# Loading, casting and transposing the first q, k group in two halves of 64 partitions

## The chip, the cores and the metric

The kernel runs on one core of one Trainium2 chip. The metric is the device time of one execution in microseconds (us); lower is better. The core has five engines with an instruction queue each: PE (TensorE, matmuls and transposes; its weight loads are shown apart as PEld), DVE (VectorE), ACT (ScalarE), POOL (GpSimd) and SP (SyncE, which issues transfers). Each engine runs its own instructions in order, and semaphores hold one engine until another has done its part.

## The reference

The reference is a block-causal attention followed by a feed-forward layer with a maximum of two branches. q, k and v have 8 batches, 8 heads, 576 positions and 64 features.

```python
def _attn_ref(q, k, v):
    B, H, S, D = q.shape                      # 8, 8, 576, 64
    block = 64
    scale = 1.0 / np.sqrt(D)
    scores = scale * np.matmul(q, k.transpose(0, 1, 3, 2))
    ...
    mask = block_i >= block_j                 # by blocks of 64 positions
    scores = np.where(mask, scores, -1000000000.0)
    ...
    attn = np.exp(scores)                     # softmax over the keys
    attn = attn / (np.sum(attn, axis=-1, keepdims=True) + 1e-09)
    return np.matmul(attn, v)

def _moe_ref(x, w1, w2, w_out):               # x: 4608 x 512
    return np.maximum(x @ w1, x @ w2) @ w_out # 512 -> 1024 -> 512
```

## The kernel before

**Units of work.** Two heads make a pair, and there are 32 pairs (`NPAIR`). Two pairs, that is four heads of one batch, make a group; there are 16 groups. A group's q and k are loaded as one tile each of 128 partitions: the partition index is `(h p)`, with `h` (0 or 1) choosing the pair and `p` running over 64 partitions, each of which holds 9 (`RPP`) consecutive positions of each of the pair's two heads. So partitions 0 to 63 belong to the first pair of the group and 64 to 127 to the second. A tile holds 1152 fp32 values in each partition.

**From q and k to scores.** `load_qk` (L89) issues the two loads of a group. `cast` (L101) turns the fp32 tile into bf16 tiles `qn` and `kn`, and its list `parts` says which engine takes which of the 9 columns. `transposes` (L259) transposes 64 x 128 pieces on PE, nine for each pair, into two PSUM tiles, and gives back a function that copies these to the SBUF tiles `qT` and `kT` of the two pairs (L272). `scores` (L278) multiplies kT by qT for the two heads of a pair.

**A pair.** `burst_a` (L295) computes two PSUM tiles of scores and issues their exponentials on ACT (L288) and block masks on POOL (L293). `burst_b` (L306) does the other two. There are two score buffers in PSUM (`ps_s`), so the first tile of burst_b waits for the first exponential of burst_a, and so on. `av` (L317) multiplies the exponentials by v and normalises on DVE, `x_out` (L345) transposes the result into `xT`, and `h_unit` and `y_unit` are the feed-forward layer, whose matmuls are dealt out by `fill` between the attention work of later pairs.

**Buffers in PSUM.** All transposes, warm-up matmuls, av and feed-forward tiles take turns in one pool of four buffers (`ps_m`, tag "m"), in the order in which the program asks for them. A tile waits until the reader of the buffer's previous tile is done.

**Order.** The order is written out by hand. The start is: the loads of groups 0, 1 and 2 from SP and ACT; memsets on DVE; the casts of group 0, split between DVE, POOL and ACT (L145, L146); three v loads on POOL, the q cast of group 1 on POOL (L149), two more v loads and four weight loads on POOL. On PE, `warm_up(16)` issues 16 matmuls on zeros, then come the 36 transposes of q and k of group 0 (L418, L419), `warm_up(3)`, and the four copies that feed the first two pairs (L421 to L424). Then the loop over the first four pairs (L425) runs: burst_a, some other work and warm-ups, burst_b. For pair 0 the other work is the k cast of group 1 on DVE and `warm_up(4)` after burst_a, and the q transposes of group 1 and `warm_up(2)` after burst_b. Steady state, with the feed-forward work mixed in, begins after these four pairs.

Of the kernel before, what the change touches and what calls it, by code (L numbers as in the profile page):

```python
# [8 lines left out]
FP32 = mybir.dt.float32  # L9
BF16 = mybir.dt.bfloat16  # L10
# [4 lines left out]
def kernel(  # L15
# [10 lines left out]
    nc = tc.nc  # L26

    B, H, S, D = q.shape
    P = 128
# [13 lines left out]
    NP = 64  # L43
    RPP = S // NP
# [17 lines left out]
    raw = ctx.enter_context(tc.tile_pool(name="raw", bufs=4))  # L62
    qkn = ctx.enter_context(tc.tile_pool(name="qkn", bufs=2))
# [4 lines left out]
    ps_m = ctx.enter_context(tc.tile_pool(name="ps_m", bufs=4, space=bass.MemoryType.PSUM))  # L68
# [5 lines left out]
    qT_r = [ring.tile([P, S], BF16, name=f"qT{r}") for r in range(NT)]  # L74
    kT_r = [ring.tile([P, S + APAD], BF16, name=f"kT{r}") for r in range(NT)]
# [6 lines left out]
    ident = wpool.tile([P, P], BF16, name="ident")  # L82


    raws = {}
    qk_n = {}
    dve, pool, act = nc.vector.tensor_copy, nc.gpsimd.tensor_copy, nc.scalar.copy

    def load_qk(g, queues, gated=False):  # L89
        b, u = divmod(g, GPB)  # L90
        for nm, src, queue in (("q", q, queues[0]), ("k", k, queues[1])):
            raws[nm, g] = t = raw.tile([P, 2, RPP * D], FP32, name=f"{nm}raw")
            if gated:
                nc.gpsimd.memset(t[:, 0, :1], 0.0)
            queue.dma_start(
                out=t[:],
                in_=src[b, 4 * u:4 * u + 4].rearrange(
                    "(s h) (p t) d -> (h p) s (t d)", h=2, t=RPP),
            )

    def cast(nm, g, parts):  # L101
        t = raws.pop((nm, g)).rearrange("p s (t d) -> p t s d", d=D)
        qk_n[nm, g] = n = qkn.tile([P, RPP, 2, D], BF16, name=f"{nm}n")
        for copy, j0, j1 in parts:
            copy(out=n[:, j0:j1], in_=t[:, j0:j1])  # L105
# [20 lines left out]
    dve, pool, act = nc.vector.tensor_copy, nc.gpsimd.tensor_copy, nc.scalar.copy  # L126
    SP, ACT = nc.sync, nc.scalar
    warm = small.tile([P, 1], FP32, name="warm")
    load_qk(0, (SP, ACT))
    nc.vector.memset(warm[:], 0.0)  # L130
    zeros = wpool.tile([P, SPAN], BF16, name="zeros")
    nc.vector.memset(zeros[:], 0.0)  # L132
# [9 lines left out]
    for r in range(NA):  # L142
        nc.vector.memset(aT_r[r][BLK:, :, CB[4] + 512:], 0.0)
        nc.vector.memset(aT_r[r][:BLK, :, AW:], 0.0)
    cast("q", 0, ((dve, 0, 6), (pool, 6, RPP)))  # L145
    cast("k", 0, ((act, 0, 5), (dve, 5, RPP)))  # L146
    for c in range(3):
        load_v(0, c)
    cast("q", 1, ((pool, 0, RPP),))  # L149
    for c in range(3, NCH):  # L150
        load_v(0, c)
# [99 lines left out]
    def warm_up(n):  # L251
        pw = ps_m.tile([P, SPAN], FP32, name="ps_w", tag="m")
        for _ in range(n):
            nc.tensor.matmul(pw[:], zeros[:, :P], zeros[:], start=True, stop=True)  # L254
# [4 lines left out]
    def transposes(nm, g, copies):  # L259
        n = qk_n.pop((nm, g))  # L260
        pts = [ps_m.tile([P, RPP, NP], BF16, name=f"ps_{nm}T", tag="m") for _ in range(2)]
        for j in range(RPP):
            for i in range(2):
                r = slice(i * NP, (i + 1) * NP)
                nc.tensor.transpose(  # L265
                    pts[i][:, j, :], n[r, j].rearrange("p s d -> p (s d)"), ident[r, r],
                )

        def copy_out(which=(0, 1)):
            for i in which:  # L270
                t = (qT_r if nm == "q" else kT_r)[(2 * g + i) % NT]
                copies[i](  # L272
                    out=t[:, :S].rearrange("q (p j) -> q p j", j=RPP),
                    in_=pts[i].rearrange("q j p -> q p j"),
                )
        return copy_out
# [18 lines left out]
    def burst_a(p):  # L295
        u0 = ps_s.tile([P, 2, 512], FP32, name="ps_s", tag="s")
        scores(p, u0, 0, 0, 0, 512)
        u1 = ps_s.tile([P, 2, 512], FP32, name="ps_s", tag="s")
        scores(p, u1, 0, 0, 512, 64)
        scores(p, u1, 64, 1, 128, 448)  # L300
        exp(p, u0, 512, 0)
        mask(p, 0)
        exp(p, u1, 512, 512)
        mask(p, 576)

    def burst_b(p):  # L306
        u2 = ps_s.tile([P, 2, 512], FP32, name="ps_s", tag="s")
        scores(p, u2, 0, 2, 256, 320)
        scores(p, u2, 320, 3, 384, 192)
        u3 = ps_s.tile([P, 2, 512], FP32, name="ps_s", tag="s")  # L310
        scores(p, u3, 0, 4, 512, 64)
        exp(p, u2, 512, 1024)
        mask(p, 1024)
        mask(p, 1344)
        exp(p, u3, 64, 1536, m=BLK)

    def av(p, ts):  # L317
        b, hp = divmod(p, HP)
        vv = vv_r[b % NV]
        a = aT_r[p % NA]  # L320
        n = len(ts)
        h0 = hp // 2 * 4 + hp % 2
        if p % 2 == 0 and ts[0] == 0:
            xps[p // 2] = xpool.tile([P, NCH, 2, 2, D], BF16, name="xp")
        xp = xps[p // 2]
        po = ps_m.tile([P, n, 2, D + 1], FP32, name="ps_o", tag="m")
        n_mm = 2 * sum(t + 1 for t in ts)
        mm = 0
        for gi, t in enumerate(ts):
            for hh in range(2):  # L330
                for c in range(t + 1):
                    a0 = CB[c] + t * P
                    nc.tensor.matmul(  # L333
                        po[:, gi, hh, :], a[:, hh, a0:a0 + P], vv[:, c, h0 + 2 * hh, :],
                        start=(mm == 0), stop=(mm == n_mm - 1),
                    )
                    mm += 1
        rec = small.tile([P, 3, 2, 1], FP32, name="rec")
        nc.vector.reciprocal(rec[:, :n, :, 0], po[:, :, :, D])  # L339
        nc.vector.tensor_mul(  # L340
            xp[:, ts[0]:ts[0] + n, :, p % 2], po[:, :, :, :D],
            rec[:, :n].to_broadcast([P, n, 2, D]),
        )
# [24 lines left out]
    def fill_of(s):  # L368
        if s >= NPAIR - LAG:
            return 27  # L370
        left = 10 - s if s < 10 else 4 - (s - 2) % 4
        return -(-max(0, ready() - KEEP) // left)


    def pool_work(s):
        g, i = divmod(s, 2)
        if s == 0:
            load_w(512, 512)
            load_qk(3, (SP, SP), gated=True)
        elif s == 1 or s == 2:  # L380
            pass
        elif s == 3:
            cast("q", 2, ((act, 0, RPP),))
            cast("k", 2, ((act, 0, RPP),))
            load_qk(4, (SP, SP), gated=True)
            for c in range(3):
                load_v(1, c)
            cast("q", 3, ((pool, 0, RPP),))
            cast("k", 3, ((pool, 0, RPP),))
            for c in range(3, NCH):  # L390
                load_v(1, c)
            load_wo(0, 4)
            load_wo(4, 4)
        elif s == 4:
            pass
        elif s == 5:
            load_qk(5, (SP, SP), gated=True)
            cast("q", 4, ((pool, 0, RPP),))
        else:
            if i == 1 and g + 3 < NG:  # L400
                load_qk(g + 3, (SP, SP), gated=True)
            if g + 1 + i < NG:
                cast("kq"[i], g + 1 + i, ((pool, 0, RPP),))
            nb, j = divmod(s + 2, HP)
            if nb < B:
                for c in ((0, 1), (2, 3), (4,), ())[j]:
                    load_v(nb, c)
# [7 lines left out]


    warm_up(16)
    cq = transposes("q", 0, (dve, act))  # L418
    ck = transposes("k", 0, (act, dve))  # L419
    warm_up(3)  # L420
    cq((0,))  # L421
    ck((0,))
    cq((1,))
    ck((1,))  # L424
    for s in range(HP):  # L425
        burst_a(s)
        if s == 0:
            cast("k", 1, ((dve, 0, RPP),))
            warm_up(4)
        elif s == 1:  # L430
            transposes("k", 1, (dve, dve))()
            warm_up(2)
        elif s == 2:
            av(0, [0, 1])
            warm_up(2)
        else:
            av(0, [2, 3, 4])
        burst_b(s)
        pool_work(s)
        if s == 0:  # L440
            transposes("q", 1, (dve, dve))()
            warm_up(2)
        elif s == 1:
            warm_up(4)
        elif s == 2:
            warm_up(3)
# [8 lines left out]
    for s in range(HP, NPAIR):  # L455
# [3 lines left out]
        n = fill_of(s)  # L459
        if s == HP:  # L460
            fill(6)
            cq = transposes("q", 2, (dve, act))
            ck = transposes("k", 2, (dve, act))
# [11 lines left out]
        if s >= HP + LAG:  # L475
            p = s - LAG
# [53 lines left out]
```

The softmax here doesn't subtract the row's maximum and nothing guards it: scores larger than these inputs give would overflow.

## Time and profile before

| | |
|---|---|
| median of 7 executions | 294.28 us (293.65 to 294.82) |
| the profiled execution, its own time | 294.85 us |
| its span, first to last instruction | 293.1 us |
| PE busy | 277.8 us, 95% of the span |
| DVE, ACT, POOL busy | 181.8, 140.2, 95.8 us |
| granted TensorE clock | 1.00 |
| first scores on PE, first exponential on ACT | 9.62 us, 10.05 us |
| first feed-forward matmul | 28.9 us |

The profile is of one execution. Times in its timeline count from the first instruction of the span. A row gives the start, the time from first to last of the merged instructions, the engine, the line, the operation, what it writes and reads, and in brackets the idle time ahead of it with the instruction or transfer that ended it. Engines overlap, so busy times do not add up to the span. A busy PE is not a PE at its peak rate, because matmuls are pipelined.

### The profile page before, as it was taken

What the parts mean: (1) busy time and instruction counts of PE and PEld (TensorE: products, weight loads), DVE (VectorE), ACT (ScalarE), POOL (GpSimd) and SP (SyncE); (2) the same over time, 40 slices, a digit from 0 to 9 for tenths busy, and PEclk for the clock granted to TensorE, in tenths of its full rate; (3) what the DMA queues carried; (4) which work ended last, traced back from release to release, by engine and by line L of the source; (5) the groups of instructions that cost most, each with busy time, mean ns of one, the idle gap of its engine ahead of it and who ended that gap; (6) DMA issues with size and microseconds to landing.
All of it is one profiled execution on the core that took longest, in us unless ns stands there. A gap on an engine that the chain in (4) does not pass through costs nothing.

```text
span 293.1 us, 7406 instructions
## 1 busy us (share of the span) xinstructions
PE 277.8 (95%) x3067; PEld 141.3 (48%) x3116; DVE 181.8 (62%) x363; ACT 140.2 (48%) x200; POOL 95.8 (33%) x236
## 2 busy tenths in 40 slices
PE   8777999999999999999999999999999999999995
PEld 2445445555555454445444545454554544444443
DVE  6627767546987676756666666666665766464530
ACT  3784587576655555554555555545555000101112
POOL 3956536725553443144324432443111000000000
PEclk9999999999999999999999999999999999999999
DMA  7999999957934792568656494455110111011104
GB/s 268 284 195 284 227 168 178 218 146 176 201 25 157 81 228 45 200 73 206 77 197 73 113 171 136 83 65 66 43 38 37 38 60 49 36 72 38 72 36 143
DMA packets 56081, 36.65 MB, mean 125 GB/s; under 512 B 38768, under 2 KB 43376, under 8 KB 56048
## 3 DMA queue, kind: packets, MB, share of 16 engines
q0 software_dynamic: 41728, 7.87, 33.4%
q1 hardware_dynamic: 13760, 27.60, 27.6%
q10 hardware_dynamic: 560, 0.72, 0.8%
q8 instruction: 24, 0.39, 0.6%
q14 instruction: 9, 0.07, 0.1%
HBM read 34.60 MB, written 9.44 MB: 150 GB/s over the span
## 4 chain that ended last, share of the span: by engine, by line
PE 90%; ACT 4%; DVE 3%; issue 2%; ACTq 0%
PE ps_h L168 42%; PE ps_y L186 20%; PE ps_o L333 11%; PE ps_s L282 8%; ACT aT L288 3%; PE ps_w L254 3%; PE ps_qT L265 2%; PE ps_kT L265 2%; PE ps_xe L353 2%; DVE xp L340 1%; PE ps_y L203 1%; DVE kT L272 1%; DVE xT L358 0%; DVE qT L272 0%; DVE rec L339 0%
## 5 line engine op out<-in xcount | busy, mean ns | idle before, releaser
L168 PE MATMUL ps_h<-xT,w_sb 128*128 128x512 bf16 x547 | 133.6, 379 | 3.5 <-issue 1.7
L288 ACT ACTIVATE aT<-ps_s 128x1024 bf16<-128x1024 f32 (+1 forms) x128 | 99.2, 832 | 53.6 <-PE ps_s L282 53.6
L168 PEld LDWEIGHTS <-w_sb 128*128 128x128 bf16 x576 | 51.8, 98 | 59.7 <-issue 6.1
L175 DVE CAST h<-ps_h 128x512 bf16<-128x512 f32 x72 | 49.7, 691 | 44.9 <-PE ps_h L168 43.6
L186 PE MATMUL ps_y<-wo_sb,g 128*128 128x512 bf16 x262 | 66.5, 379 | 1.0 <-issue 0.2
L293 POOL MEMSET aT<- 64x128 bf16 x128 | 23.7, 200 | 121.9 <-ACT aT L288 121.7
L192 ACT COPY y<-ps_y 128x512 f32<-128x512 f32 x35 | 20.5, 587 | 83.9 <-PE ps_y L186 56.8
L177 DVE TENSOR_TENSOR g<-h,ps_h 128x512 bf16<-128x512 bf16 x72 | 49.3, 685 | 10.2 <-PE ps_h L168 10.2
L333 PEld LDWEIGHTS <-aT 128*128 128x128 bf16 x960 | 33.6, 98 | 14.9 <-DVE xp L340 8.4
L333 PE MATMUL ps_o<-vv,aT 128*128 128x65 bf16 x960 | 39.7, 194 | 1.1 <-DVE xp L340 0.4
L186 PEld LDWEIGHTS <-g 128*128 128x128 bf16 x280 | 25.5, 98 | 27.9 <-issue 3.2
L282 PE MATMUL ps_s<-qT,kT 64*128 64x64 bf16 (+4 forms) x384 | 34.4, 275 | 3.3 <-ACT aT L288 3.2
L109 POOL DMA_DIRECT2D vv<-in_v_dram x40 | 33.7, 848 | 0.3 <-issue 0.3
L340 DVE TENSOR_TENSOR xp<-ps_o,rec 128x256 bf16<-128x256 f32 x64 | 31.4, 491 | 2.2
L282 PEld LDWEIGHTS <-kT 64*128 64x128 bf16 x384 | 16.5, 94 | 18.9 <-issue 13.2
L339 DVE RECIPROCAL rec<-ps_o 128x4 f32<-128x4 f32 x64 | 11.8, 185 | 18.9 <-PE ps_o L333 18.8
L105 POOL CAST qn<-qraw 128x1152 bf16<-128x1152 f32 (+1 forms) x15 | 17.1, 1138 | 4.5 <-DMA qraw<-in_q_dram 4.4
L272 DVE COPY qT<-ps_qT 128x576 bf16<-128x576 bf16 x17 | 12.8, 757 | 7.2 <-PE ps_qT L265 6.0
L358 DVE COPY xT<-ps_xe 128x640 bf16<-128x640 bf16 x16 | 7.8, 490 | 12.4 <-PE ps_xe L353 12.1
L272 DVE COPY kT<-ps_kT 128x576 bf16<-128x576 bf16 x17 | 12.8, 757 | 4.3 <-PE ps_kT L265 3.2
L105 POOL CAST kn<-kraw 128x1152 bf16<-128x1152 f32 x13 | 14.9, 1145 | 1.6 <-DMA kraw<-in_k_dram 0.8
L254 PE MATMUL ps_w<-zeros 128*128 128x512 bf16 x34 | 11.7, 480 | 1.9 <-DVE zeros L132 1.2
(39 smaller groups left out, 103.0 us busy)
## 6 DMA issues: line engine op xcount, KB each, us to landing
qraw<-in_q_dram SPq DMA_DIRECT2D x16, 576.0 KB, 4.1
out_dram<-y SPq DMA_DIRECT2D x35, 256.0 KB, 2.1
kraw<-in_k_dram SPq DMA_DIRECT2D x15, 576.0 KB, 5.5
vv<-in_v_dram POOLq DMA_DIRECT2D x32, 128.0 KB, 5.9
w_sb<-in_moe_w_dram POOLq DMA_DIRECT2D x4, 256.0 KB, 8.2
w_sb<-in_moe_w_dram POOLq DMA_DIRECT2D x2, 512.0 KB, 16.2
wo_sb<-in_moe_w_out_dram POOLq DMA_DIRECT2D x2, 512.0 KB, 11.2
kraw<-in_k_dram ACTq DMA_DIRECT2D x1, 576.0 KB, 5.3
```

Of the source, the lines that this page charges most:

```text
L105: copy(out=n[:, j0:j1], in_=t[:, j0:j1])
L109: nc.gpsimd.dma_start(out=vv_r[b % NV][:rows, c, :, :D], in_=v[b, :, c * P:c * P + rows, :].rearrange("h p d -> p h d"),)
L168: nc.tensor.matmul(pt[:], w_sb[:, c, f * P:(f + 1) * P], xT[:, c, t0:t0 + SPAN], start=(c == 0), stop=(c == NDM - 1),)
L175: nc.vector.tensor_copy(out=h1[:], in_=pt[:])
L177: nc.vector.tensor_max(g[:, f, :], h1[:], pt[:])
L186: nc.tensor.matmul(py[:], g[:, f, s * P:(s + 1) * P], wo_sb[:, f, :], start=(f == 0), stop=(f == NFF - 1),)
L272: copies[i](out=t[:, :S].rearrange("q (p j) -> q p j", j=RPP), in_=pts[i].rearrange("q j p -> q p j"),)
L282: nc.tensor.matmul(ps[:m, hh, col:col + w], kT[r, c * P:c * P + m], qT[r, q0:q0 + w], start=True, stop=True,)
L288: nc.scalar.activation(out=aT_r[p % NA][:m, :, a0:a0 + w], in_=ps[:m, :, :w], func=AF.Exp, scale=scale,)
L293: nc.gpsimd.memset(aT_r[p % NA][BLK:, :, a0:a0 + BLK], 0.0)
L333: nc.tensor.matmul(po[:, gi, hh, :], a[:, hh, a0:a0 + P], vv[:, c, h0 + 2 * hh, :], start=(mm == 0), stop=(mm == n_mm - 1),)
L340: nc.vector.tensor_mul(xp[:, ts[0]:ts[0] + n, :, p % 2], po[:, :, :, :D], rec[:, :n].to_broadcast([P, n, 2, D]),)
```

## The change

The first group is no longer handled by `load_qk`, `cast` and `transposes`, but by three functions of its own, which treat the two pairs (`h` = 0 and 1, partitions 0 to 63 and 64 to 127) one after the other. The loads become four transfers of 64 partitions each, in the order q h=0 (SP), k h=0 (ACT), q h=1 (SP), k h=1 (ACT). The casts of h=0 keep the split of before. The q cast of h=1 goes to POOL, ahead of the v loads, and the k cast of h=1 to DVE, behind the copy of the first qT. Only the transposes of h=0 stay ahead of the first scores; those of h=1 move behind burst_a of pair 0. Each takes one PSUM buffer instead of two, and the copy of the second qT moves from ACT to DVE.

```diff
+    def load_first():
+        t = {nm: raw.tile([P, 2, RPP * D], FP32, name=f"{nm}raw") for nm in "qk"}
+        for h in range(2):
+            for nm, src, queue in (("q", q, nc.sync), ("k", k, nc.scalar)):
+                queue.dma_start(
+                    out=t[nm][h * NP:(h + 1) * NP],
+                    in_=src[0, :4].rearrange("(s h) (p t) d -> h p s (t d)", h=2, t=RPP)[h],
+                )
...
+    def cast_first(nm, h, parts):
...
+        r = slice(h * NP, (h + 1) * NP)
+        for copy, j0, j1 in parts:
+            copy(out=n[r, j0:j1], in_=t[r, j0:j1])
+
+    def transposes_first(nm, h, copy):
...
+        pt = ps_m.tile([P, RPP, NP], BF16, name=f"ps_{nm}T", tag="m")
+        for j in range(RPP):
+            nc.tensor.transpose(
+                pt[:, j, :], n[r, j].rearrange("p s d -> p (s d)"), ident[r, r])
+        t = (qT_r if nm == "q" else kT_r)[h]
+        copy(
+            out=t[:, :S].rearrange("q (p j) -> q p j", j=RPP),
+            in_=pt.rearrange("q j p -> q p j"),
+        )
...
-    load_qk(0, (SP, ACT))
+    load_first()
...
-    cast("q", 0, ((dve, 0, 6), (pool, 6, RPP)))
-    cast("k", 0, ((act, 0, 5), (dve, 5, RPP)))
+    cast_first("q", 0, ((dve, 0, 6), (pool, 6, RPP)))
+    cast_first("k", 0, ((act, 0, 5), (dve, 5, RPP)))
+    cast_first("q", 1, ((pool, 0, RPP),))
     for c in range(3):
         load_v(0, c)
     cast("q", 1, ((pool, 0, RPP),))
...
     warm_up(16)
-    cq = transposes("q", 0, (dve, act))
-    ck = transposes("k", 0, (act, dve))
+    transposes_first("q", 0, dve)
+    transposes_first("k", 0, act)
+    cast_first("k", 1, ((dve, 0, RPP),))
     warm_up(3)
-    cq((0,))
-    ck((0,))
-    cq((1,))
-    ck((1,))
     for s in range(HP):
         burst_a(s)
         if s == 0:
+            transposes_first("q", 1, dve)
+            transposes_first("k", 1, dve)
             cast("k", 1, ((dve, 0, RPP),))
             warm_up(4)
```

The second argument of `cast_first` and `transposes_first` is the half `h` of group 0; that of `cast` is the group.

More of the change, by code (lines that the diff above doesn't have):

```diff
@@ L99, in load_qk @@
             )
+    def load_first():
[6 more added lines that the diff above has]
+                )
+        for nm in "qk":
+            raws[nm, 0] = t[nm]
+            qk_n[nm, 0] = qkn.tile([P, RPP, 2, D], BF16, name=f"{nm}n")
+    def cast_first(nm, h, parts):
+        t = raws[nm, 0].rearrange("p s (t d) -> p t s d", d=D)
+        n = qk_n[nm, 0]
+        r = slice(h * NP, (h + 1) * NP)
+        for copy, j0, j1 in parts:
+            copy(out=n[r, j0:j1], in_=t[r, j0:j1])
+    def transposes_first(nm, h, copy):
+        n = qk_n[nm, 0]
+        r = slice(h * NP, (h + 1) * NP)
+        pt = ps_m.tile([P, RPP, NP], BF16, name=f"ps_{nm}T", tag="m")
[7 more added lines that the diff above has]
+        )
     def cast(nm, g, parts):
```

## The prediction

> **What bounds the kernel now.** I read the page first, then the chain of waits, then the timeline of the first 24 us. The page says that PE carries the run as a whole:
>
> ```profile
> PE 277.8 (95%) x3067; PEld 141.3 (48%) x3116; DVE 181.8 (62%) x363; ACT 140.2 (48%) x200; POOL 95.8 (33%) x236
> PE 90%; ACT 4%; DVE 3%; issue 2%; ACTq 0%
> ```
>
> The change touches only the first dozen microseconds. PE runs its instructions in a fixed order, so a shift that survives the start moves the whole run by as much. No row behind the start waits for a transfer long enough to hold it: the first MoE matmul waits at 28.86 us for the DVE copy of xT, and its weights, issued at 11.96 us with about 7 us to land, are there long before. So the question is one shift in microseconds, read from the timeline (start, duration, engine, work):
>
> ```profile
> 1.23 6.43 PE L254 MATMUL ps_w<-zeros 128*128 128x512 bf16 x16 [1.23 <-DVE zeros L132]
> ...
> 5.71 0.56 DVE L105 CAST qn<-qraw 128x768 bf16<-128x768 f32 x1
> 5.74 0.89 POOL L105 CAST qn<-qraw 128x384 bf16<-128x384 f32 x1 [4.43 <-DMA qraw<-in_q_dram]
> ...
> 6.19 0.73 DVE L105 CAST kn<-kraw 128x512 bf16<-128x512 f32 x1
> ...
> 6.58 2.77 POOL L109 DMA_DIRECT2D vv<-in_v_dram  x3
> ...
> 7.59 0.44 PE L265 MATMUL ps_qT<-ident,qn 64*128 64x64 bf16 x18
> ...
> 8.06 0.76 DVE L272 COPY qT<-ps_qT 128x576 bf16<-128x576 bf16 x1 [1.15 <-PE ps_qT L265]
> ...
> 8.32 0.64 ACT L272 COPY kT<-ps_kT 128x576 bf16<-128x576 bf16 x1 [1.52 <-PE ps_kT L265]
> ...
> 8.88 0.81 PE L254 MATMUL ps_w<-zeros 128*128 128x512 bf16 x2 [0.58 <-DVE qT L272]
> ...
> 9.33 1.18 POOL L105 CAST qn<-qraw 128x1152 bf16<-128x1152 f32 x1
> 9.40 1.34 DVE L105 CAST kn<-kraw 128x1152 bf16<-128x1152 f32 x1
> ...
> 9.62 0.61 PE L282 MATMUL ps_s<-qT,kT 64*128 64x512 bf16 x6
> ```
>
> The reader is to see three things. First, q has landed by 5.74 and all casts of the first group end by 6.92 (6.19 + 0.73), yet the transposes start at 7.59, when the 16 warm-up matmuls let PE go (1.23 + 6.43 = 7.66). An earlier load gains nothing at this point. Second, the first scores (9.62) stand behind three more warm-up matmuls on PE, and those begin at 8.88 because they need a PSUM buffer that the copy of qT frees (8.06 + 0.76 = 8.82). Third, POOL goes from its part of the cast through three v loads to the q cast of group 1, which ends at 9.33 + 1.18 = 10.51. From the first scores on, PE and ACT alternate:
>
> ```profile
> 10.05 3.00 ACT L288 ACTIVATE aT<-ps_s 128x1024 bf16<-128x1024 f32 x4 [0.54 <-PE ps_s L282]
> ...
> 12.04 0.21 PE L282 MATMUL ps_s<-qT,kT 64*128 64x64 bf16 x2 [0.52 <-ACT aT L288]
> ...
> 12.06 0.44 PE L265 MATMUL ps_qT<-ident,qn 64*128 64x64 bf16 x18
> ```
>
> The second exponential frees the scores at 12.04, and the group 1 transposes follow at once: they use the POOL cast of 10.51 with 1.5 us to spare.
>
> [...] a POOL cast of 384 took 0.89 us beside the DVE cast of 768 that took 0.56, while a whole 1152 took 1.18. [...] No large 64-partition load is in this trace. [...]
>
> **The change part by part.**
>
> *Loads.* Two transfers of 576 KB become four of 288 KB. SP and ACT each issue one more (about 0.49 us each): the later SP loads and ACT's table load (1.27, used by the exponential at 10.05) go back by half a microsecond. The table load has 7 us of cover. The group 1 loads, which landed at about 7.5 (q) and 9 us (k), are cast at 9.33 and 9.40 now, and later after the change. The first halves are there well before 5.7. The DVE memsets end at 5.73, so its casts don't start sooner.
>
> *Casts.* A cast costs by elements in a partition, so halving the partitions halves nothing: the h=1 casts are added work, 1152 for q on POOL (1.1 to 1.18 us) and 1152 for k on DVE ([...]1.34 at worst).
>
> *Front of PE.* Nine transposes per tensor instead of eighteen. Eighteen take 7.87 - 7.59 = 0.28 us to start, so nine take 0.14. qT ends at 7.59 + 0.14 + 0.19 (one transpose) = 7.92, its DVE copy at 7.94 + 0.76 = 8.70. kT ends at 8.06, its ACT copy at 8.08 + 0.64 = 8.72. Each transpose now takes one PSUM buffer instead of two, so the three warm-ups get the fourth of four buffers and needn't wait: from 7.87, three of 0.21 are over at 8.50. The scores start at 8.77 instead of 9.62: **0.85 us earlier**. Exponentials run 9.20 to 11.15, and the two last score matmuls come at 11.20 instead of 12.04.
>
> *DVE behind it.* [...] The h=1 transposes sit behind the first scores (about 9.35 and 9.45), then four warm-ups to about 10.4, then scores that ACT wants at 11.15. Copies of qT (moved here from ACT) and kT: 9.7 to 11.2. Cast of k of group 1, then the copies of group 1 from about 12.0, where they now start at 12.52. [...] If the h=1 cast takes 1.34, the scores are ready at 11.5 and the group 1 copies start near 12.9, and the gain shrinks to about 0.1. [...]
>
> *POOL behind it.* This decides. Let E be the end of the q cast of h=1. Three v loads and the group 1 cast took 10.51 - 6.58 = 3.93 us. The group 1 transposes can start at E + 3.93 + 0.05, and the alternation gets there at 11.20. So E up to 7.2 keeps all of the gain; E = 8.06 gives it all back; beyond that each microsecond is lost in full, since burst_a of pair 1 and its exponentials stand behind these transposes on PE. When does q, h=1 land? The packets in the trace say that q's last packet went at 5.0 us and k's near 5.45, with about 0.6 us more until the casts started. [...] I take the middle, 6.0. [...] the POOL cast runs 6.2 to 7.3, and DVE's k cast ends at about 7.6, just before PE needs it at 7.73. The cast of k, h=1 falls among the v loads; loads there took 0.92 each beside DVE casts and 0.88 at 24 us without, so I add 0.1. The transposes start at 7.3 + 3.93 + 0.1 + 0.05 = 11.38 instead of 12.04: **-0.66 us**. The mask memsets of pair 0 move by as much as POOL (15.01 to about 15.9) and are wanted near 16.4: covered. The v loads landed 6 to 7 us after issue, some 3 us ahead of use: covered.
>
> The profiled execution took 294.85 us with a span of 293.1; its sum becomes 294.2. It is 0.57 above the median of 294.28, so against the median: **293.6**.
>
> **The rivals.** *Half given back:* E between 7.5 and 8.1[...]. The wait for the copy of qT is replaced by PE waiting for POOL's cast; gain 0.1 to 0.5, time about 294.0. [...] *Slower:* the halves serialize at some 200 GB/s. Then 1.18 MB last 5.9 us from 1.6, q h=1 lands about 7.7, E is 8.85, [...] the group 1 transposes start at 12.9 to 13.5: 0.9 to 1.4 us late, 295.2 to 295.7. It decides from E = 8.65 (0.6 us late). Against: SP's queue starts 0.8 us ahead of ACT's, so the two are often on different halves. *It does nothing:* if a warm-up or another wait still puts the scores at 9.6, only the added work remains, and most is covered: 294.3.
>
> **How the numbers follow.** 0.2% (0.6 us) is about what a measurement of this kernel can tell from no change. The gain kept (-0.5 to -0.85): 0.50, nearly all of it over 0.2%. Half given back or nothing done: 0.33. Slower as above: 0.17. So faster 0.48, within 0.2% 0.34, slower 0.18. The likeliest case by itself spans 293.4 to 293.9. The range that holds 8 in 10 reaches 293.3 below and 294.9 above.
>
> **What would show it.** Right: three warm-ups starting near 7.9, first scores near 8.8, first exponential near 9.2, POOL's group 1 cast ending by about 11.4, the exponential of pair 1 near 12.7 instead of 13.40. Wrong: PE waiting for POOL's qn ahead of the group 1 transposes for over half a microsecond; a DVE cast of k h=1 near 1.3 us; q h=1 landing after 6.6; or the first scores unmoved.

## The result, and the profile after

The changed kernel takes 298.14 us (median of 12 executions, 295.53 to 299.48) against 294.27 us for the kernel before (31 executions). The ratio is 1.0131, with a 95% interval of 1.0114 to 1.0149: **slower by 1.3%**, or 3.9 us. The prediction was 293.6 us, in a range of 293.3 to 294.9. It was wrong.

The profiled execution of the changed kernel took 297.75 us with a span of 296.0. Its timeline, in the same columns as before:

```profile
0.74 1.38 SPq L106 DMA_DIRECT2D qraw<-in_q_dram  x2
0.75 1.64 ACTq L106 DMA_DIRECT2D kraw<-in_k_dram  x2
...
4.55 0.50 POOL L119 CAST qn<-qraw 64x384 bf16<-64x384 f32 x1 [3.24 <-DMA qraw<-in_q_dram]
...
7.59 0.43 PE L126 MATMUL ps_qT<-ident,qn 64*128 64x64 bf16 x9
...
7.87 0.42 PE L126 MATMUL ps_kT<-ident,kn 64*128 64x64 bf16 x9
8.06 0.76 DVE L129 COPY qT<-ps_qT 128x576 bf16<-128x576 bf16 x1 [1.59 <-PE ps_qT L126]
...
8.22 0.82 PE L288 MATMUL ps_w<-zeros 128*128 128x512 bf16 x3
...
9.02 0.61 PE L316 MATMUL ps_s<-qT,kT 64*128 64x512 bf16 x6
9.45 1.94 ACT L322 ACTIVATE aT<-ps_s 128x1024 bf16<-128x1024 f32 x2 [0.49 <-PE ps_s L316]
9.52 1.15 POOL L119 CAST qn<-qraw 64x1152 bf16<-64x1152 f32 x1 [4.47 <-DMA qraw<-in_q_dram]
9.59 1.35 DVE L119 CAST kn<-kraw 64x1152 bf16<-64x1152 f32 x1 [0.77 <-DMA kraw<-in_k_dram]
...
13.43 1.14 POOL L138 CAST qn<-qraw 128x1152 bf16<-128x1152 f32 x1
...
14.63 0.44 PE L299 MATMUL ps_qT<-ident,qn 64*128 64x64 bf16 x18 [1.87 <-POOL qn L138]
...
15.96 3.00 ACT L322 ACTIVATE aT<-ps_s 128x1024 bf16<-128x1024 f32 x4 [2.02 <-PE ps_s L316]
```

The front works as intended: the first half of q is there at 4.55, the three warm-ups follow the transposes at once, and the first exponential starts at 9.45 instead of 10.05. Then POOL's row of 9.52 says what went wrong: it sat idle for 4.47 us until the second half of q landed. Behind it on POOL come the three v loads and the group 1 cast, which ends at 13.43 + 1.14 = 14.57. PE stood for 1.87 us until that cast let the group 1 transposes go, at 14.63 instead of 12.06. The exponential of pair 1 starts at 15.96 instead of 13.40, 2.56 us late. In the kernel before, the rows of group 1's first copies and of this exponential are:

```profile
12.52 1.42 DVE L272 COPY qT<-ps_qT 128x576 bf16<-128x576 bf16 x2 [1.77 <-PE ps_qT L265]
...
13.40 3.00 ACT L288 ACTIVATE aT<-ps_s 128x1024 bf16<-128x1024 f32 x4 [0.36 <-PE ps_s L282]
```

The chain of waits over the first 32 us leads back to that transfer (start, duration, what held the end):

```profile
1.53 7.87 DMA qraw<-in_q_dram
...
9.52 1.15 POOL qn L119
10.67 0.27 POOL vv L142
...
13.43 1.15 POOL qn L138
...
14.63 0.44 PE ps_qT L299 x18
```

The shift is carried unchanged. The first copy of y on ACT comes at 59.2 us instead of 56.7, the last at 290.7 instead of 288.2. Of the 2.9 us between the two spans, 2.5 are there at the last copy of y; the other 0.35 or so lies behind the last output transfers, whose issue ends at 290.87 in the one and 293.39 in the other; its cause is open.

Why is the second half late? The transfers of the window 3.5 to 5.5 us, first in the kernel before, then in the changed one (packets, bytes, and the time that packets took as a share of 16 DMA engines; q1 is SP's queue, q10 is ACT's):

```profile
DMA packets 369, 0.79 MB, mean 397 GB/s; under 512 B 24, under 2 KB 24, under 8 KB 369
...
q10 hardware_dynamic: 211, 0.47, 59.7%
q1 hardware_dynamic: 158, 0.33, 42.5%
```

```profile
DMA packets 202, 0.43 MB, mean 213 GB/s; under 512 B 17, under 2 KB 17, under 8 KB 202
...
q10 hardware_dynamic: 120, 0.24, 61.9%
q1 hardware_dynamic: 82, 0.19, 41.6%
```

The DMA engines are as busy in both (102% and 104%), but the changed kernel moves little more than half the bytes. Leaving out the small packets, 2.04 us of engine time for each of the 16 gave 345 packets before and 2.07 us gave 185 after: 95 ns a packet against 179 ns.

### The profile page after: what moved, and what is told of

Its sections match the earlier page's. It is cut to its first block, busy times and chain, and to the rows that moved or that the text cites. A ratio compares the mean times of both kernels' runs of the same rounds, so it can differ in the third digit from the quotient of the medians.

```text
span 296.0 us, 7414 instructions
## 1 busy us (share of the span) xinstructions
PE 278.5 (94%) x3067; PEld 141.7 (48%) x3116; DVE 183.5 (62%) x365; ACT 139.7 (47%) x199; POOL 96.5 (33%) x237
## 3 DMA queue, kind: packets, MB, share of 16 engines
q0 software_dynamic: 41728, 7.87, 33.5%
## 4 chain that ended last, share of the span: by engine, by line
PE 86%; ACT 3%; DMA 3%; DVE 3%; issue 2%; POOL 1%; SPq 0%; ACTq 0%; POOLq 0%
PE ps_h L202 42%; PE ps_y L220 20%; PE ps_o L367 11%; PE ps_s L316 7%; ACT aT L322 3%; DMA qraw<-in_q_dram 3%; PE ps_qT L299 2%; PE ps_kT L299 2%; PE ps_xe L387 2%; DVE xp L374 1%; PE ps_w L288 1%; POOL vv L142 1%; PE ps_y L237 1%; DVE kT L306 1%; POOL qn L138 0%
## 5 line engine op out<-in xcount | busy, mean ns | idle before, releaser
L316 PEld LDWEIGHTS <-kT 64*128 64x128 bf16 x384 | 16.4, 94 | 18.4 <-issue 12.5
L138 POOL CAST qn<-qraw 128x1152 bf16<-128x1152 f32 x14 | 16.1, 1153 | 0.1
L392 DVE COPY xT<-ps_xe 128x640 bf16<-128x640 bf16 x16 | 7.8, 490 | 12.4 <-PE ps_xe L387 12.1
L306 DVE COPY qT<-ps_qT 128x576 bf16<-128x576 bf16 x16 | 12.0, 757 | 5.3 <-PE ps_qT L299 4.2
L306 DVE COPY kT<-ps_kT 128x576 bf16<-128x576 bf16 x16 | 12.0, 757 | 4.3 <-PE ps_kT L299 3.2
```

What stands on the lines that cost most here:

```text
L306: copies[i](out=t[:, :S].rearrange("q (p j) -> q p j", j=RPP), in_=pts[i].rearrange("q j p -> q p j"),)
L316: nc.tensor.matmul(ps[:m, hh, col:col + w], kT[r, c * P:c * P + m], qT[r, q0:q0 + w], start=True, stop=True,)
```

## The experiments

Three theories were set against each other. **Ports:** a transfer whose partitions all lie in 0 to 63 or 64 to 127 runs at half the rate (the name is only a label; what lies behind such a rate was not shown). **Count:** more and smaller transfers are slow by themselves. **Order:** the casts added on POOL and DVE cost the time wherever the data is.

**Whole loads, the rest of the change kept.**

```diff
-        for h in range(2):
-            for nm, src, queue in (("q", q, nc.sync), ("k", k, nc.scalar)):
-                queue.dma_start(out=t[nm][h * NP:(h + 1) * NP], in_=...[h])
+        for nm, src, queue in (("q", q, nc.sync), ("k", k, nc.scalar)):
+            queue.dma_start(out=t[nm][:], in_=...)      # as load_qk
```

> Edit: the changed kernel with one change undone, the first q and k tiles are loaded whole again (one transfer of 128 partitions each); casts, transposes and order stay as changed. Ports theory (the halves of 64 partitions load at half the rate and the second half comes late): q and k land near 5.7 and 6.1 us, the q cast of h=1 ends on POOL near 7.4, the first exponential of pair 1 starts near 12.7 to 13.1 instead of 15.96, and the time is 293.5 to 294.1, at or under that of before. Order theory (the added casts on POOL and DVE ahead of the v loads and the group 1 cast cost the time wherever the data is): the group 1 q cast still ends beyond 13 us and the time stays above 296.

Measured: 294.69 us, ratio 1.0016 (1.0005 to 1.0027). Nearly all of the loss is gone with this one edit, so it is the loads. But no gain appears either. From its timeline:

```profile
5.88 2.17 POOL L118 CAST qn<-qraw 64x384 bf16<-64x384 f32 x2 [4.57 <-DMA qraw<-in_q_dram]
...
7.90 1.35 DVE L118 CAST kn<-kraw 64x1152 bf16<-64x1152 f32 x1
...
8.29 0.61 PE L315 MATMUL ps_s<-qT,kT 64*128 64x512 bf16 x6
...
10.73 1.35 DVE L137 CAST kn<-kraw 128x1152 bf16<-128x1152 f32 x1
10.81 1.15 POOL L137 CAST qn<-qraw 128x1152 bf16<-128x1152 f32 x1
...
12.01 0.44 PE L298 MATMUL ps_qT<-ident,qn 64*128 64x64 bf16 x18 [0.95 <-POOL qn L137]
...
13.35 3.00 ACT L321 ACTIVATE aT<-ps_s 128x1024 bf16<-128x1024 f32 x4 [1.10 <-PE ps_s L315]
```

With the data on time, the first scores start at 8.29. Part of that is not the data: in this execution the warm-ups let PE go at 6.49 us, in the two profiles above at 7.59. POOL's two casts end at 5.88 + 2.17 = 8.05 and its group 1 cast at 11.96, PE waits 0.95 us for it, and the exponential of pair 1 is back at 13.35, as in the profile of before (13.40), although PE started 1.1 us sooner. With a start as early, the order of before reaches 12.46 (the last section has that profile). So POOL's chain holds this kernel near 13.35 however early PE is let go, which fits the times: its 13 executions begin at 294.49, those of the kernel before at 293.65. The order theory is wrong for the loss, and right about where the gain goes.

**The half loads alone, in the kernel before.**

```diff
-    load_qk(0, (SP, ACT))
...
+    for h in range(2):
+        for nm, src, queue in (("q", q, SP), ("k", k, ACT)):
+            queue.dma_start(out=raws[nm, 0][h * NP:(h + 1) * NP], in_=...[h])
```

> Edit: the kernel before with one change made, the first q and k tiles are loaded as four transfers of 64 partitions in the order of the changed kernel; casts and transposes stay whole. Ports theory: the last half lands near 9.5 us, so all casts of the first group and with them the first transposes come near 10.4 instead of 7.6 us; POOL's v loads and group 1 cast go back by 3 to 4 us; time 297 to 298.5. Order theory: the loads alone cost little, 294 to 294.8.

Measured: 297.93 us, ratio 1.0122 (1.0092 to 1.0152). The loads alone make almost the whole loss.

```profile
7.59 0.89 POOL L105 CAST qn<-qraw 128x384 bf16<-128x384 f32 x1 [6.29 <-DMA qraw<-in_q_dram]
...
8.78 0.72 ACT L105 CAST kn<-kraw 128x640 bf16<-128x640 f32 x1 [4.87 <-DMA kraw<-in_k_dram]
...
11.55 3.00 ACT L295 ACTIVATE aT<-ps_s 128x1024 bf16<-128x1024 f32 x4 [0.32 <-PE ps_s L289]
...
14.91 3.00 ACT L295 ACTIVATE aT<-ps_s 128x1024 bf16<-128x1024 f32 x4 [0.36 <-PE ps_s L289]
```

The data landed earlier here than in the changed kernel (q in time for casts at 7.56, k for casts at 8.78; I had expected the last near 9.5), and the exponential of pair 1 is 1.5 us late, not 2.6. The traces have 16 completion marks for each transfer and say where the difference lies: here all 16 of q, h=1 came by 7.46; in the changed kernel 14 came by 7.23 and the last two at 8.38 and 9.39. The run with filled gaps below, which has the changed kernel's loads, repeats this: 15 by 7.47, the last at 9.47. With whole loads the 16 marks of the first q lie within 0.7 us of each other. What held the stragglers is open, and so is whether they come in every execution. Yet the time is as long: in this profiled execution the granted TensorE clock was 0.50 from 30 to 32 us, of which more below.

**Each queue keeps to one half.** SP takes h=0 of q and of k, ACT takes h=1 of both.

```diff
-        for h in range(2):
-            for nm, src, queue in (("q", q, nc.sync), ("k", k, nc.scalar)):
+        for nm, src in (("q", q), ("k", k)):
+            for h, queue in ((0, nc.sync), (1, nc.scalar)):
```

> Edit: the changed kernel with its four 64-partition transfers dealt out otherwise: SP takes h=0 of q, then of k, ACT takes h=1 of q, then of k, so that the two queues always work on different partition halves. Ports theory: the rate in the window 3.5 to 5.5 us goes from 200 to about 400 GB/s, all four halves land by 6.3 us, q h=1 by about 5; time 293.4 to 294.1. Count theory (it is the smaller and more numerous transfers, with their longer issue, that are slow): the rate stays near 200 GB/s, the last half lands near 9.5 us, time 297.5 to 298.5.

Measured: 296.24 us, ratio 1.0075 (1.0042 to 1.0109), and the rate stayed at 227 GB/s from 3.5 to 5.5 us. The ports theory as I had put it failed: two halves in flight do not add up. The queues by themselves show what happened instead, from 3.5 to 4.5 us and then from 5 to 6 us:

```profile
q10 hardware_dynamic: 99, 0.23, 101.5%
q1 hardware_dynamic: 14, 0.01, 4.3%
```

```profile
q1 hardware_dynamic: 103, 0.23, 102.1%
q10 hardware_dynamic: 7, 0.01, 5.7%
```

For a microsecond nearly all engine time goes to ACT's queue (q10), then nearly all to SP's (q1). The half transfers run one after the other. A half transfer is 128 packets of 2304 bytes; why the engines stay with one queue that long was not shown. The time is better than the change's because both halves of q now come first: POOL's cast of the second ends at 7.26, not at 10.67.

One half transfer was not slow. From 3.0 to 3.5 us, while SP's queue sends the first half of q, the same profile has:

```profile
DMA packets 88, 0.19 MB, mean 378 GB/s; under 512 B 6, under 2 KB 6, under 8 KB 88
...
q1 hardware_dynamic: 81, 0.17, 94.1%
```

In all four profiles with half loads, the changed kernel's among them, the packets of the first half transfer took 93 ns in the median, and those of the three behind it 173 to 192 ns. It landed about 1.1 us after its last packet began, where a whole q took 0.6 us before the change. Why the first one is spared is open.

**Four transfers of 288 KB, each over all 128 partitions.**

```diff
+        for s in range(2):                       # one of the pair's two heads
...
+                    out=t[nm][:, s],
+                    in_=src[0, 2 * s:2 * s + 2].rearrange("h (p t) d -> (h p) (t d)", t=RPP),
```

> Edit: the changed kernel with four transfers of the same size as in the change, but each of all 128 partitions and one of the two heads. Ports theory: about 400 GB/s, everything landed by 6.3 us; q is complete near 5.8; time 293.5 to 294.3. Count theory: as slow as the change, last landing near 9.5 us, 297.5 to 298.5.

Measured: 295.21 us, ratio 1.0039 (1.0025 to 1.0053), 0.9 us above the range that I gave for ports, but the window 3.5 to 5.5 us is back at full rate:

```profile
DMA packets 404, 0.81 MB, mean 404 GB/s; under 512 B 53, under 2 KB 53, under 8 KB 404
```

Same number and size of transfers, full rate: the count theory is out. Each of these transfers, too, reads only two of the four heads (here neighbours), so reading fewer heads at a time is not the cause either. The 0.5 us over the run with whole loads were not followed up.

**The first half taken from the middle.** Partitions 32 to 95 first, then 0 to 31, then 96 to 127.

```diff
+        for p0, p1 in ((NP // 2, P - NP // 2), (0, NP // 2), (P - NP // 2, P)):
...
+                    out=t[nm][p0:p1], in_=...[p0:p1],
```

> Edit: the changed kernel with its first tiles loaded in another cut: first partitions 32 to 95 (64 partitions across the middle) of q on SP and of k on ACT, then 0 to 31, then 96 to 127. Ports theory (a transfer is slow because its partitions all lie in one half, 0 to 63 or 64 to 127): the packets of the first pair of transfers take about 93 ns each and the rate up to 4 us is as in the kernel before (from 226 towards 400 GB/s); the transfers of 32 partitions behind them run near 200 GB/s. Count theory (fewer than 128 partitions is slow by itself): the first pair stays near 200 GB/s with about 187 ns a packet, and those of 32 partitions are slower still, near 100. The time is not the point; casts of h=0 wait for parts of two transfers.

Measured: 295.99 us (one execution). The windows 3.0 to 4.5 us and 4.5 to 6.5 us:

```profile
DMA packets 297, 0.59 MB, mean 392 GB/s; under 512 B 42, under 2 KB 42, under 8 KB 297
```

```profile
DMA packets 245, 0.46 MB, mean 228 GB/s; under 512 B 47, under 2 KB 47, under 8 KB 245
```

Sixty-four partitions across the middle run at 392 GB/s, and the pieces of 32 that follow, each inside one half, at 228. Not 100, as it would be if the rate went by the number of partitions. Nor is it that the middle pieces came first: the second of them, on SP's queue until 4.3 us, took 93 ns a packet too, where the second half transfer took 175 to 187 in the other runs. So, behind the first transfer, it is where the partitions lie that counts; why was not shown.

**Whole loads, with two repairs.** The DVE casts of 9 columns become 8 and 1, and only two v loads stand ahead of POOL's group 1 cast.

```diff
-    for c in range(3):
+    for c in range(2):
         load_v(0, c)
     cast("q", 1, ((pool, 0, RPP),))
-    for c in range(3, NCH):
+    for c in range(2, NCH):
...
-    cast_first("k", 1, ((dve, 0, RPP),))
+    cast_first("k", 1, ((dve, 0, 8), (dve, 8, RPP)))
...
-            cast("k", 1, ((dve, 0, RPP),))
+            cast("k", 1, ((dve, 0, 8), (dve, 8, RPP)))
```

> Edit: as the run with whole loads, and two more: the DVE casts of k of 9 columns are issued as 8 columns and 1, and only two v loads instead of three stand ahead of the group 1 q cast on POOL. [...] The group 1 q cast on POOL then ends 0.9 us earlier (near 11.05), the first exponential of pair 1 starts near 12.5 instead of 13.35 to 13.4, and the time is 0.6 to 0.9 us under that of before (ratio 0.997 to 0.998). If the order of the first pair is worth nothing, the ratio stays at 1.000 to 1.002.

Measured: 294.30 us, ratio 0.9998 (0.9984 to 1.0013). POOL's group 1 cast ended at 11.27, but:

```profile
8.01 2.08 POOL L141 DMA_DIRECT2D vv<-in_v_dram  x2
...
8.92 1.20 DVE L118 CAST kn<-kraw 64x1024 bf16<-64x1024 f32 x2
...
11.60 1.50 DVE L137 CAST kn<-kraw 128x1024 bf16<-128x1024 f32 x2
...
13.21 3.00 ACT L321 ACTIVATE aT<-ps_s 128x1024 bf16<-128x1024 f32 x4 [0.32 <-PE ps_s L315]
```

The split casts took 1.20 and 1.50 us in sum beside POOL's v loads, once a little less and once a little more than the 1.35 of a whole one. Taken singly, the 8 columns of h=1 took 0.69 us, half of what 9 take, but the one column left took 0.59; for group 1 it was 0.99 and 0.58. So 8 columns cost less than 9 both times, but the one column left took nearly 0.6 us, and the split lost again what it gained. The expected 12.5 became 13.21.

**The same two repairs in the kernel before.** Its casts of group 1 and v loads were edited as in the run above; the first group stayed whole.

> Edit: the kernel before with only the two extra edits of the run before this one (DVE cast of k of group 1 as 8 and 1 columns, two v loads ahead of the group 1 q cast); loads, casts and transposes of the first group stay whole. The group 1 casts had 1.5 us of slack in the kernel before, so both theories give a ratio of 0.999 to 1.001; a gain here would say that the gain of the other run is not due to the halves of the first group.

Measured: 294.36 us, ratio 1.0005 (0.9989 to 1.0021): nothing, as expected.

**Filling PE's gaps in the changed kernel.**

```diff
+            warm_up(5)
             transposes_first("q", 1, dve)
...
+            warm_up(7)
             transposes("q", 1, (dve, dve))()
```

> Edit: the changed kernel with 12 more warm-up matmuls on zeros in the two stretches in which PE waits for POOL: 5 ahead of the transposes of q h=1, 7 ahead of those of q of group 1. If the time beyond the 2.55 us of late start (298.1 against 296.8) comes from a TensorE clock that drops after these idle stretches, the clock is 1.000 in nearly all executions and the median is 296.6 to 297.2. If the drop comes from elsewhere, for instance the DVE-bound stretch at 26 to 31 us, the clock still is below 1 in most executions and the median stays near 298.

Measured: 297.82 us (297.44 to 298.13, 4 executions), ratio 1.0113 (1.0086 to 1.0141). Neither of the two cases that I had set out came: three of the four executions had a clock of 0.999 or 1.000, against three of twelve of the changed kernel, but the time did not fall to 297. The profiled execution had clock 1.000 and still took 297.82 with a span of 296.0, the changed kernel's own. At full clock, idle PE at 10 and 14 us is not what costs beyond the late start; whether filling it keeps the clock up, four executions cannot say.

**Two attempts to free the chain.** Both load whole and keep two v loads ahead of POOL's group 1 cast; the group 1 cast on DVE is issued as 6 columns and 3. In one the k cast of h=1 moves to ACT, in the other q of h=1 is split between ACT and POOL.

```diff
+    cast_first("k", 1, ((act, 0, RPP),))                 # first run
...
+    cast_first("q", 1, ((act, 0, 5), (pool, 5, RPP)))    # second run
...
+            cast("k", 1, ((dve, 0, 6), (dve, 6, RPP)))
```

> Edit: whole loads, as in the first run; the k cast of h=1 moves from DVE to ACT, ahead of the copy of the first kT, where ACT stood idle from about 6.9 to 8.3 us; two v loads ahead of the group 1 q cast; the DVE cast of k of group 1 as 6 columns and 3. If POOL's chain and the 1.35 us cast on DVE were what held the run with whole loads at no gain, the first exponential of pair 1 starts at 12.4 to 12.8 and the ratio is 0.997 to 0.999. If the early first scores are worth nothing because the next limit (the DVE copies of group 1, near 12.5 us) takes over, the exponential starts near 12.6 but the third tile of pair 1 is late by as much, and the ratio is 0.999 to 1.001.

> Edit: whole loads; the q cast of h=1 is split, 5 columns on ACT and 4 on POOL; k of h=1 stays on DVE as 9 columns; two v loads ahead of the group 1 q cast; the DVE cast of k of group 1 as 6 columns and 3. POOL's group 1 cast then ends near 10.2 us, ahead of all demand. If POOL's chain alone held the run with whole loads, the first exponential of pair 1 starts near 12.5 and the ratio is 0.997 to 0.999. If the DVE chain behind it (1.35 us cast, two copies, cast, two copies) is the next limit, the exponentials of burst_b wait for it and the ratio is 0.999 to 1.001.

Measured: 294.20 us, ratio 1.0013 (0.9997 to 1.0029), and 294.22 us, ratio 1.0001 (0.9988 to 1.0014). In the first, the exponential of pair 1 came at 13.13, where 12.4 to 12.8 was expected. In the second, POOL's group 1 cast ended at 10.49, ahead of all demand, and the exponential of pair 1 still came at 13.45:

```profile
8.77 1.35 DVE L118 CAST kn<-kraw 64x1152 bf16<-64x1152 f32 x1
...
11.60 1.42 DVE L137 CAST kn<-kraw 128x768 bf16<-128x768 f32 x2
...
12.95 1.41 DVE L305 COPY qT<-ps_qT 128x576 bf16<-128x576 bf16 x2
13.02 0.61 PE L315 MATMUL ps_s<-qT,kT 64*128 64x512 bf16 x6 [0.29 <-DVE kn L137]
13.45 3.00 ACT L321 ACTIVATE aT<-ps_s 128x1024 bf16<-128x1024 f32 x4 [0.32 <-PE ps_s L315]
```

Now DVE is next: its copies of group 1 start at 12.95, where they started at 12.52 before the change. No version beat the kernel before.

## Why the prediction was wrong

**When the second half lands: the step that failed.** I counted q, h=1 at 5.65 to 6.4 us and took 6.0, on the grounds that the two queues would often be on different halves and so add up. No trace had shown that, nor the rate of a load of 64 partitions. It landed at 9.39, in time for a cast at 9.52. Behind the first transfer, the halves took turns at about 200 GB/s (213 from 3.5 to 5.5 us). The first packets also went late, at 2.25 us where I had counted from 1.6, and the two issues took 1.38 us on SP and 1.64 on ACT instead of about 0.98. So far this is my slower rival, which had 7.7 us: 14 of the 16 marks came by 7.23, and with the same loads in the kernel before all came by 7.46. The last two marks, at 8.38 and 9.39, are beyond every case that I had. By the sum of the next paragraph, a landing at 7.46 would have started the group 1 transposes near 12.7, some 0.7 us late instead of 2.57 (an estimate). An execution of the changed kernel at full clock took 295.53 us, two others 296.95 and 297.75; stragglers in some executions and not in others would explain that, but only the last was profiled. That the halves run one after the other I had put into that rival, with 0.17.

**What follows from E: right.** I wrote that the group 1 transposes start at E + 3.93 + 0.05, with E the end of the q cast of h=1. In the changed kernel E = 9.52 + 1.15 = 10.67 gives 14.65; measured 14.63. With whole loads E = 8.05 gives 12.03; measured 12.01. The 0.1 us that I had added for the v loads was not needed. That each microsecond beyond 8.06 is lost in full holds too: E is 2.61 us beyond it, the transposes are 2.57 late and the last copy of y 2.5.

**The front: right, but too large.** The scores moved to 9.02, not 8.77. Nine transposes took as long as eighteen, 0.28 us from q's first to k's first (7.59 to 7.87) in both kernels. In the kernel before they alternated between the two pairs, on partitions 0 to 63 and 64 to 127, and leaving out every other one saved nothing. The exponential gained 0.60 instead of 0.85. The buffer argument held: three warm-ups at 8.22, with no wait. The sum also took the end of the 16 warm-ups from one profile (7.66 us) as given; that it moves, and what follows, is in the last section.

**The DVE cast of k, h=1: taken too short.** I took about half of the 1.34 us in the trace, as if only POOL's cast beside it made the group 1 cast slow; no trace had shown that. It is 1.34 or 1.35 in every profile in which DVE casts 9 columns, of 64 partitions or of 128, beside POOL's cast (1.15, undisturbed) and beside its v loads. Casts of 6 columns took 0.49 and of 4 columns 0.41 with POOL idle, and 8 columns took 0.69 in the run with two repairs. Why 9 columns take so much longer than 8 was not shown. I had named what 1.35 would do, a gain of about 0.1, and that is where the runs with whole loads ended.

**The size of the loss.** Between the two profiled executions lie 297.75 - 294.85 = 2.90 us. Between the medians lie 3.87, because the profiled execution of before stood 0.58 above its median and that of after 0.39 below. The former fits its late warm-ups (last section). The latter goes with the clock: of the 12 executions after, three had a granted clock of 1.000 (median 296.95 us) and nine had 0.983 to 0.994 (median 298.88 us). Where the clock fell is seen in other kernels' profiles only: to 0.50 at 30 to 32 us with the half loads alone, and to 0.50 at 28 to 30 us in the run with two repairs and in the first attempt to free the chain. With the half loads alone PE waits there for DVE's normalisation (0.46 us ahead of 29.09) and copies (0.37 us ahead of 30.41). What brings it about is open.

## What to carry to other kernels

Cut a load so that each piece still spans both halves of the partitions; here pieces inside 0 to 63 or 64 to 127 took nearly twice the time per packet (179 ns against 95), all but the first (93 ns), and a second queue did not win it back (227 GB/s against 397 with whole loads). Before an early first half is counted as a gain, follow the engine that casts the second half: whatever is queued behind that cast in order inherits its wait. And a gain at the head of a chain is worth only the slack of the next engine in it, here POOL's, then DVE's. Before the starts of two profiles are compared, see when the warm-ups ended in each: here that alone moved a start by 0.9 us.

## What the runs showed of the hardware that was not expected

- A packet of 2304 bytes takes 95 ns of an engine's time when the transfer spans all partitions and 179 ns when it lies in one half, except in the first half transfer of a run (93 ns); two queues on different halves do not add up (227 GB/s against 397).
- Of the 16 completion marks of a half transfer, one or two came 1 to 2 us after the others in two of four profiles with half loads (9.39 against 7.23 us). With whole loads those of the first q all came within 0.7 us.
- A DVE cast of 1152 fp32 to bf16 in 9 columns takes 1.35 us, and POOL's cast beside it takes no longer than usual (1.15); as 8 and 1 columns beside POOL's v loads it took 1.20 to 1.50.
- The time at which the 16 warm-up matmuls let PE go varies between executions with the same warm-ups: the first transposes start at 7.59 in the kernel before, and at 6.65 in the profile of the run that edits only its group 1 casts and v loads, whose start is otherwise the same. The warm-ups follow each other 0.43 us apart until 6.75 in the one and until 5.04 in the other, and then 0.21 us apart; what sets that moment is open. The second profile:

```profile
6.65 0.44 PE L265 MATMUL ps_qT<-ident,qn 64*128 64x64 bf16 x18
...
9.10 3.00 ACT L288 ACTIVATE aT<-ps_s 128x1024 bf16<-128x1024 f32 x4 [0.47 <-PE ps_s L282]
...
12.46 3.00 ACT L288 ACTIVATE aT<-ps_s 128x1024 bf16<-128x1024 f32 x4 [0.36 <-PE ps_s L282]
```

With casts done by 6.9 us, the kernel before can use such a start: the first exponential comes at 9.10, earlier than the change's 9.45, and that of pair 1 at 12.46 instead of 13.40. The two profiled executions took 293.92 and 294.85 us, which is as far apart. This is a likely reason for the spread of its own executions from 293.65 to 294.94, of which one alone was profiled.
